# Shorter first passes over two blocks, one stay for the sigmoids, and a reordered opening

## The chip, the core and the metric

The kernel runs on one core of a Trainium2 chip. The metric is the device time of one execution in microseconds (us). A core has a matrix engine (PE, with PEld for its weight loads), a vector engine (DVE), an activation engine (ACT), GpSimd (POOL) and a queue engine (SP) that issues the DMAs. Every engine works through its own list of instructions in order; they meet only at semaphores. A difference of about 2% (9 us) is what is called a change in the verdicts.

## The reference

An attention of the mLSTM kind over 768 steps for 2 batches and 8 heads of width 40 gives 1536 rows of 320 numbers. Two feed-forward layers of width 2048 follow, each with its own weights:

```python
h_tilde = np.einsum('bhde,bhe->bhd', C, qt)
denom = np.maximum(np.abs(nq), 1.0)
o = 1.0 / (1.0 + np.exp(-o_gate[:, :, t]))
y[:, :, t] = o * h_tilde / denom
...
h = x @ w_in
g = h - np.tanh(h)            # layer 1
x = g @ w_out
...
h = x @ w_in
g = h * np.tanh(log1p(exp(h)))  # layer 2
return g @ w_out
```

## The kernel before

The 1536 rows are twelve tiles of 128, in six blocks of two. The 2048 columns of a layer are 16 weight parts of 128. A part comes in by DMA as `raw` and is made ready by `conv_w` in six passes: on DVE a shift (L198), on ACT the sign (a Prelu, L206), on DVE a shift-and-or (L210), on ACT the high half (L213), on DVE the low half (L215, L216). Every product uses high and low halves, so the first product of one part for one block is 8 matmuls of 256 columns (L538, tile `h`), and the second is 6 matmuls of 320 columns (L598, L599, L600, tile `acc`): `gh` times the high weights, `gh` times the low, and `gl` times the high.

Two parts make a tile of work (`tile1`). ACT takes two Tanh of `h` (L560, L561), a Square (L562), a Relu (L565) and the rounded half `gh` (L549); DVE makes `g` (L563), `t` (L564) and a predicated copy (L566); POOL makes `gl` (L550).

Layer 1 visits every block twice. The first pass over block n uses `CUT[n]` parts, starting as soon as the attention of that block is done, and while it runs the attention of block n+1 is computed beside it. After the sixth block a second pass visits each block with the parts that are left. What a first pass leaves out, the second does: the sum of matmuls doesn't depend on `CUT`. Layer 2 follows.

The attention of a row tile j goes: `nb` (PE) to an Exp (`Dm`, ACT L340), a mask (POOL L342), scores `sc` (PE), their product (DVE L362), `it` and `pv` (PE L369, L380), then DVE's sums and the gate (L374 to L394). L393 multiplies by the sigmoid of the output gate, which `session` puts on ACT (L259); the Sigmoid needs another activation table than the Exp, and so a table load (ACT_TABLE_LOAD) on either side. The gated rows `xo` are transposed (`xt`, PE L283), and ACT and DVE make the halves of `xT` (L285, L286), which the first products of that block read. Below, "a" and "b" are the two row tiles of block 1, and parts and tiles of work are counted from 0.

The order on each engine comes from a scheduler that ranks ready instructions by its own timing model; `with after(...)` only puts an instruction behind another. In the opening, where PE would stand idle, `keep(n, x)` puts n filler matmuls (`w_ps`, L639) behind x.

Of the kernel before, what the change touches and what calls it, by code (L numbers as in the profile page):

```python
# [8 lines left out]
F32 = mybir.dt.float32  # L9
F32R = mybir.dt.float32r  # L10
U32 = mybir.dt.uint32
AF = mybir.ActivationFunctionType
# [13 lines left out]
def kernel(  # L26
# [54 lines left out]
    NB = len(blocks1)  # L81


    CUT = [8] + [10] * (NB - 1)
    M1 = max(BLOCKS) * L
    M2 = max(len(x) for x in flat) * L
    MX = max(NP * M1, M2)
# [38 lines left out]

    last, chain, fill, mark, second = [], [], [], [], []

    texp, tbl, dls, tanhs = [], [], [], []

    scored, gated, rounded, relus = {}, {}, {}, {}

# [24 lines left out]
    def copy_r(eng, o, x):  # L157
        if eng == 0:
            nc.scalar.activation(out=o, in_=x, func=AF.Copy)
        elif eng == 1:  # L160
            nc.vector.tensor_copy(o, x)
        else:
            nc.gpsimd.tensor_scalar(o, in0=x, scalar1=1.0, scalar2=0.0, op0=ALU.mult, op1=ALU.add)
# [6 lines left out]
    def load_w(n=1):  # L170
        for _ in range(n):
            if pending_loads:
                layer, f = pending_loads.pop(0)
                early = layer == 0 and f < ER
                t = (xp if early else rawp).tile(
                    [P, 2 * WC], U32, tag="x" if early else "raw", name="raw", bufs=NB - 1 if early else None
                )
                queued(
                    lambda: nc.sync.dma_start(out=t, in_=(w1, w2)[layer][f].bitcast(U32)), layer == 0 and f < CUT[0]
                )  # L180
                raw[layer, f] = t
# [3 lines left out]
    def conv_w(layer, f, first=(), behind=()):  # L185
        r = raw.pop((layer, f)).rearrange("p (n t) -> p n t", t=2)
        lo32, z = r[:, :, 0], r[:, :, 1]
        zf = z.bitcast(F32)
        w = wp.tile([P, WT], F32R, tag="w", name="w")
        wf = w.bitcast(F32)  # L190

        head = texp if (layer, f) == (0, 0) else tanhs if layer == 0 and f < CUT[0] else []
        if layer == 0 and f:
            head = head + [scaled[0, f - 1]]
        with after(first):
            nc.vector.tensor_scalar(lo32, in0=lo32, scalar1=29, scalar2=None, op0=ALU.logical_shift_right)  # L198
        if second:
            nc.vector.scalar_tensor_tensor(  # L200
                lo32, in0=z, scalar=0x80000000, in1=lo32, op0=ALU.bitwise_and, op1=ALU.bitwise_or
            )
            scaled[layer, f] = nc.scalar.activation(out=zf, in_=zf, func=AF.Copy, scale=2.0 ** -111)
        else:
            with after(head):
                scaled[layer, f] = nc.scalar.activation(  # L206
                    out=zf, in_=zf, func=AF.Prelu, scale=2.0 ** -111, alpha=-2.0 ** 32
                )
        with after(behind):
            third[layer, f] = nc.vector.scalar_tensor_tensor(  # L210
                z, in0=z, scalar=3, in1=lo32, op0=ALU.logical_shift_left, op1=ALU.bitwise_or
            )
        cvd[:] = [nc.scalar.activation(out=w[:, 0:WC], in_=zf, func=AF.Copy)]  # L213
        eng = nc.gpsimd if (layer, f) == (0, 0) else nc.vector
        eng.tensor_tensor(w[:, WC:WT], in0=zf[:, 0:REM0], in1=wf[:, 0:REM0], op=ALU.subtract)  # L215
        lows[layer, f] = eng.tensor_tensor(w[64:P, REM0:REM1], in0=zf[64:P, REM0:REM1], in1=wf[64:P, REM0:REM1], op=ALU.subtract)  # L216
        wtile[layer, f] = w
# [60 lines left out]
    def transpose_x(layer, bi, pos):  # L278
        j = blk[layer, bi][pos]
        src = xo[:, j, :]  # L280
        t_ps = at_ps([P, 3, P], "xt")
        for n in range(3):
            x = nc.tensor.transpose(t_ps[:, n, :], src[:, n * P:(n + 1) * P], ident)  # L283
        hi, lo = (t[:, :, pos * L:(pos + 1) * L] for t in xT[layer, bi])
        chain[:] = [x, nc.scalar.activation(out=hi, in_=t_ps, func=AF.Copy)]  # L285
        chain.append(nc.vector.tensor_tensor(lo, in0=t_ps, in1=hi.bitcast(F32), op=ALU.subtract))  # L286

    def trans(layer, bi):
        new_xT(layer, bi)
        for n in range(len(blk[layer, bi])):  # L290
            transpose_x(layer, bi, n)
            yield

    def keep(n, x):
        if fill:
            fill[0](n, [x])

    def attention(j):
# [80 lines left out]
        for h in range(H):  # L379
            x = nc.tensor.matmul(pv[:, h, :], lhsT=Dm[:, h, :], rhs=v[:, h, :], start=True, stop=True)  # L380
        if not j:
            keep(2, x)
        if c > 0:
            nc.vector.tensor_tensor(hv, in0=hv, in1=pv, op=ALU.add)
        else:
# [13 lines left out]
        if c + 1 < NCH:  # L399
            st = at_ps([P, HG, D1], "st")  # L400
            with in_turn(first=chain[:1] if c == 0 else ()) as turn:
                for h in [HG * r + g for g in range(HG) for r in range(2)]:
                    turn(lambda: nc.tensor.matmul(hp(st, h), lhsT=k[:, h, :], rhs=wv[:, h, :], start=True, stop=True))
            for r in range(2):
                sl = slice(HP * r, HP * r + D)
                if c == 0:
                    copy_r(0, C[sl, :, r, :], st[sl])
                else:
                    dc = dec[sl, b, :, c:c + 1].to_broadcast([D, HG, D1])
                    nc.gpsimd.tensor_tensor(C[sl, :, r, :], in0=C[sl, :, r, :], in1=dc, op=ALU.mult)  # L410
                    nc.vector.tensor_tensor(C[sl, :, r, :], in0=C[sl, :, r, :], in1=st[sl], op=ALU.add)
# [141 lines left out]
    def tile1(i):  # L553
        l, bi, fs, nt = span(i)
        n = len(fs) * nt
        h = hps.pop(i)
        u, t, g = (g2.tile([P, MX], F32, tag=nm, name=nm)[:, 0:n] for nm in "utg")

        with after([scaled[0, fs[-1] + 1]] if i < CUT[0] // NP - 1 else []):
            nc.scalar.activation(out=u, in_=h, func=AF.Tanh, scale=G_B)  # L560
            tanhs[:] = [nc.scalar.activation(out=t, in_=h, func=AF.Tanh)]  # L561
        nc.scalar.activation(out=u, in_=u, func=AF.Square, scale=G_SA)  # L562
        mark[:] = [nc.vector.tensor_tensor(g, in0=u, in1=h, op=ALU.mult)]  # L563
        nc.vector.tensor_tensor(t, in0=h, in1=t, op=ALU.subtract)  # L564
        relus[i] = nc.scalar.activation(out=u, in_=u, func=AF.Relu, bias=bias[:, 0:1])  # L565
        nc.vector.copy_predicated(out=g, mask=u.bitcast(U32), data=t)  # L566
        split_g(i, g, n)
# [64 lines left out]
    def program():  # L632
# [64 lines left out]
        def go(g, n=1):  # L697
            for _ in range(n):
                next(g, 0)
# [2 lines left out]
        rest = rest()  # L702
        go(gb, 4)
        go(ga)
        transpose_x(0, 0, 0)
        go(gb)
        keep(4, chain[0])
        transpose_x(0, 0, 1)
        go(ga)
        go(gb)  # L710
        load_w(2)
        loads_to(2 * B, "qk")
        load_w(1)
        loads_to(2 * B, "kv")
        load_w(1)
        start = chain[:]
        conv1 = [0]

# [10 lines left out]
                conv1[0] += 1  # L729

        lead1(PRE)
        rest = rest()
        rest = rest()
        at_pools[:] = [(ps_acc, "acc")] * PS[0] + [(ps_at, "at")] * PS[2]
# [2 lines left out]
        def attend():  # L737
            for k in range(1, NB):
                js = blk[0, k]
                gens = [(n, attention(j)) for n, j in enumerate(js)]  # L740
                if k < NB - 1:
                    new_xT(0, k)
                loads_to(js[0] + 1)
                while gens:
                    for n, g in list(gens[:2]):
                        loads_to(js[n] + 2)
                        if next(g, 0) == 0:
                            gens.remove((n, g))
                            if k < NB - 1:
                                yield  # L750
                                transpose_x(0, k, n)
                        yield
            left.close()
            late["x"] = pool(left, "lateX", 1, reuse_waits="tile")
            late["A"] = pool(left, "lateA", 2, reuse_waits="tile")
            yield from trans(0, NB - 1)
# [35 lines left out]
        n_s = CUT[0] // NP  # L792


        CY, R2, E2 = 6, 3, 6

        def conv_to(i, bi, f):
            if i < n_s:
# [12 lines left out]
        for i in range(len(tiles)):  # L811
# [28 lines left out]
            mm1(i)  # L840
            if l == 0:
                tile1(i)
                if 1 < i < 4:
                    session(2 * i - 3, 2 * i - 1 + (i > 2), i == 3, [cvd[0], relus[2]] if i < 3 else [rounded[2], relus[3], rounded[3]])
                qm.append(i)
                if len(qm) > LAG:
                    mm2(qm.pop(0))
                if i:
                    ahead(min(int(14 * (k + (i - i0 + 1) / n_seg + 0.4)), (8, 14)[i - 1] if i < 3 else 14 * NB))
                if k >= T2:  # L850
                    next(sg, None)
                    next(sg, None)
            else:
                tile2(i)
                qm.append(i)
                if len(qm) > LAG2:
                    mm2(qm.pop(0))
                next(sg, None)
# [66 lines left out]
```

## Time and profile before

| | us |
|---|---|
| three runs | 457.56, 459.34, 546.25 |
| their median | 459.34 |
| the profiled execution | 457.39 |
| its span, first to last instruction | 455.4 |
| PE busy | 444.0 (97%) |
| PE's filler matmuls, 45 of them | 14.7 |
| DVE busy | 299.9 (66%) |
| ACT busy | 284.2 (62%) |

The run of 546.25 is a stray one and is not compared with. The profiled execution's time is 1.99 us above its span. Busy times are sums over one engine, so they overlap between engines; PE's contains the fillers. The granted clock is what PE ran at as a share of 2.4 GHz: 1.00 is 2.4 GHz and 0.50 is 1.2 GHz.

### The profile page before, as it was taken

To read this page: it belongs to the slowest core of one execution; us is meant where nothing else is said; L and a number is where in the kernel's file an instruction comes from. 1 tells how busy PE (TensorE), PEld (TensorE's weight loads), DVE (VectorE), ACT (ScalarE), POOL (GpSimd) and SP (SyncE) were. 2 spreads that over 40 slices of the span, in tenths; PEclk is the share of its full clock that TensorE was granted. 3 is DMA by queue.
4 is the path that set the end of the run, shared out by engine and by line. 5 is a ranking of instruction groups with operands and counts; after the bars stand their busy time and mean duration, and the time that the engine had idled before them with its cause. 6 is when DMAs were issued, how large, how long until landed. Compare 5 with 4: busy or idle time off the path is not lost. (4 is left out here: it accounts for less than half of the span.)

```text
span 455.4 us, 7958 instructions
## 1 busy us (share of the span) xinstructions
PE 444.0 (97%) x3099; PEld 403.0 (88%) x3099; DVE 299.9 (66%) x524; ACT 284.2 (62%) x519; POOL 105.1 (23%) x119
## 2 busy tenths in 40 slices
PE   9989989999999999999999999999999999999997
PEld 5756979989989999999999989999989899898996
DVE  7889889948988687568799986989622212211112
ACT  6679798568584866789778877676533332322331
POOL 2305534433464421243323332000000000000000
PEclk9799999999999999999999999999999999999999
DMA  7984644531344310001111110435010000010001
GB/s 239 374 286 163 184 108 139 167 97 47 105 131 123 94 64 1 1 2 63 65 65 63 65 64 1 134 121 189 2 59 0 1 0 2 15 44 0 1 0 58
DMA packets 22728, 38.03 MB, mean 84 GB/s; under 512 B 1348, under 2 KB 17028, under 8 KB 22692
## 3 DMA queue, kind: packets, MB, share of 16 engines
q1 hardware_dynamic: 22692, 37.54, 25.7%
q8 instruction: 24, 0.39, 0.4%
q14 instruction: 12, 0.10, 0.1%
HBM read 35.41 MB, written 1.97 MB: 82 GB/s over the span
## 5 line engine op out<-in xcount | busy, mean ns | idle before, releaser
L538 PE MATMUL h<-xT,w 128*128 128x256 f32 (+1 forms) x1152 | 205.9, 321 | 4.9 <-ACT w L213 1.9
L538 PEld LDWEIGHTS h<-xT,w 128*128 128x128 f32 x1152 | 167.9, 189 | 21.9 <-ACT w L213 2.3
L598 PE MATMUL acc<-w,gh 128*128 128x320 f32 x384 | 119.7, 313 | 0.5 <-DVE xo L615 0.5
L599 PE MATMUL acc<-w,gh 128*128 128x320 f32 x384 | 118.8, 310 | 0.0
L600 PE MATMUL acc<-w,gl 128*128 128x320 f32 x384 | 114.8, 312 | 0.0
L550 POOL TENSOR_TENSOR gl<-g,gh 128x512 fp32r<-128x512 f32 x48 | 64.4, 1343 | 132.4 <-ACT gh L549 132.1
L579 DVE TENSOR_TENSOR gl<-g,gh 128x512 fp32r<-128x512 f32 x48 | 33.2, 691 | 88.1 <-ACT g L578 88.0
L577 ACT ACTIVATE gh<-h 128x512 fp32r<-128x512 f32 x48 | 28.8, 600 | 75.4 <-PE h L538 75.3
L598 PEld LDWEIGHTS acc<-w,gh 128*128 128x128 f32 x384 | 72.2, 188 | 3.0 <-ACT u L562 0.7
L599 PEld LDWEIGHTS acc<-w,gh 128*128 128x128 f32 x384 | 72.2, 188 | 2.4
L600 PEld LDWEIGHTS acc<-w,gl 128*128 128x128 f32 x384 | 70.3, 188 | 1.0 <-POOL Dm L342 0.4
L563 DVE TENSOR_TENSOR g<-u,h 128x512 f32<-128x512 f32 x48 | 32.8, 684 | 25.2 <-ACT u L562 16.9
L566 DVE COPY_PREDICATED g<-u,t 128x512 f32<-128x512 uint32 x48 | 40.1, 843 | 12.8 <-ACT u L565 12.7
L549 ACT ACTIVATE gh<-g 128x512 fp32r<-128x512 f32 x48 | 30.4, 634 | 18.9 <-DVE g L566 17.1
L565 ACT ACTIVATE u<-u,bias 128x512 f32<-128x512 f32 x48 | 34.7, 726 | 6.9 <-DVE g L563 6.8
L213 ACT ACTIVATE w<-raw 128x704 fp32r<-128x704 f32 x32 | 27.3, 860 | 15.0 <-DVE raw L210 14.8
L564 DVE TENSOR_TENSOR t<-h,t 128x512 f32<-128x512 f32 x48 | 32.9, 685 | 0.0
L560 ACT ACTIVATE u<-h 128x512 f32<-128x512 f32 x48 | 28.6, 595 | 4.1 <-PE h L538 3.7
L562 ACT ACTIVATE u<-u 128x512 f32<-128x512 f32 x48 | 30.5, 639 | 0.0
L210 DVE SCALAR_TENSOR_TENSOR raw<-raw 128x704 uint32<-128x704 uint32 x32 | 29.1, 921 | 0.5
L561 ACT ACTIVATE t<-h 128x512 f32<-128x512 f32 x48 | 28.8, 599 | 0.0
L578 ACT ACTIVATE g<-h 128x512 f32<-128x512 f32 x48 | 28.6, 596 | 0.0
(104 smaller groups left out, 452.5 us busy)
## 6 DMA issues: line engine op xcount, KB each, us to landing
raw<-in_w_dram SPq DMA_DIRECT2D x32, 704.0 KB
qk_t<-in_qk_dram SPq DMA_DIRECT2D x12, 512.0 KB
kv_t<-in_kv_dram SPq DMA_DIRECT2D x12, 324.0 KB
out_dram<-xo SPq DMA_DIRECT2D x12, 160.0 KB
xo<-in_og_dram SPq DMA_DIRECT2D x2, 800.0 KB
xo<-in_og_dram SPq DMA_DIRECT2D x1, 320.0 KB
sd<-nr SPq DMA_DIRECT2D x20, 4.0 KB
md<-nr SPq DMA_DIRECT2D x10, 8.0 KB
```

Of the source, the lines that this page charges most:

```text
L538: y = nc.tensor.matmul(t[:, k * nt:(k + 1) * nt], lhsT=w[:, o:o + P], rhs=x[:, kk, :], start=(n == 0), stop=(n == len(pairs) - 1),)
L549: rounded[i] = nc.scalar.activation(out=gh, in_=g, func=AF.Copy)
L550: nc.gpsimd.tensor_tensor(gl, in0=g, in1=gh.bitcast(F32), op=ALU.subtract)
L562: nc.scalar.activation(out=u, in_=u, func=AF.Square, scale=G_SA)
L563: mark[:] = [nc.vector.tensor_tensor(g, in0=u, in1=h, op=ALU.mult)]
L564: nc.vector.tensor_tensor(t, in0=h, in1=t, op=ALU.subtract)
L565: relus[i] = nc.scalar.activation(out=u, in_=u, func=AF.Relu, bias=bias[:, 0:1])
L566: nc.vector.copy_predicated(out=g, mask=u.bitcast(U32), data=t)
L579: mark.append(nc.vector.tensor_tensor(gl, in0=g, in1=gh.bitcast(F32), op=ALU.subtract))
L598: turn(lambda: nc.tensor.matmul(a, lhsT=gh[:, sl], rhs=wh, start=(f in ends_), stop=False))
L599: turn(lambda: nc.tensor.matmul(a, lhsT=gh[:, sl], rhs=wl, start=False, stop=False))
L600: turn(lambda: nc.tensor.matmul(a, lhsT=gl[:, sl], rhs=wh, start=False, stop=end))
```

## The change

The first pass over block 0 uses 6 parts where it used 8, the one over block 1 uses 8 where it used 10 (`CUT`); the second pass takes over the difference. The pace at which later parts are converted starts from 4 where it started from 6 (`CY`). The five later sigmoids, which stood in two calls of `session` behind tiles 2 and 3, stand in one call behind tile 2, each behind another instruction of ACT. In the opening, three fillers stand behind the first `pv` where there were two; the sign pass of a part stands behind the Square of the tile, where it stood behind the second Tanh; the low half of the first `xT` waits for the gated rows of the second row tile; the copies of the state `C` stand behind the conversion of part 1; and the rest of block 0's attention is written after the conversion of the first two parts.

```diff
-    CUT = [8] + [10] * (NB - 1)
+    CUT = [6, 8] + [10] * (NB - 2)
...
-        head = texp if (layer, f) == (0, 0) else tanhs if layer == 0 and f < CUT[0] else []
+        head = texp if (layer, f) == (0, 0) else squared if layer == 0 and f < CUT[0] else []
...
-        chain.append(nc.vector.tensor_tensor(lo, in0=t_ps, in1=hi.bitcast(F32), op=ALU.subtract))
+
+        def low():
+            chain.append(nc.vector.tensor_tensor(lo, in0=t_ps, in1=hi.bitcast(F32), op=ALU.subtract))
+
+        return low
...
-            keep(2, x)
+            keep(3, x)
...
-                    copy_r(0, C[sl, :, r, :], st[sl])
+                    with after(cvd):
+                        copy_r(0, C[sl, :, r, :], st[sl])
...
-            tanhs[:] = [nc.scalar.activation(out=t, in_=h, func=AF.Tanh)]
-        nc.scalar.activation(out=u, in_=u, func=AF.Square, scale=G_SA)
+            nc.scalar.activation(out=t, in_=h, func=AF.Tanh)
+        squared[:] = [nc.scalar.activation(out=u, in_=u, func=AF.Square, scale=G_SA)]
...
-        transpose_x(0, 0, 0)
+        low = transpose_x(0, 0, 0)
         go(gb)
         keep(4, chain[0])
-        transpose_x(0, 0, 1)
-        go(ga)
-        go(gb)
-        load_w(2)
-        loads_to(2 * B, "qk")
-        load_w(1)
-        loads_to(2 * B, "kv")
-        load_w(1)
+        with after([gated[1]]):
+            low()
+        transpose_x(0, 0, 1)()
...
         lead1(PRE)
+        go(ga)
+        go(gb)
+        load_w(2)
+        loads_to(2 * B, "qk")
+        load_w(1)
+        loads_to(2 * B, "kv")
+        load_w(1)
...
-        CY, R2, E2 = 6, 3, 6
+        CY, R2, E2 = 4, 3, 6
...
-                if 1 < i < 4:
-                    session(2 * i - 3, 2 * i - 1 + (i > 2), i == 3, [cvd[0], relus[2]] if i < 3 else [rounded[2], relus[3], rounded[3]])
+                if i == 2:
+                    session(1, NCH, True, [cvd[0], rounded[1], relus[2], rounded[2], rounded[2]])
```

In the changed kernel the line numbers after the first edits are 4 to 7 higher (L538 is L543, L598 is L603, L380 is L384, L562 is L567).

On ACT, around the sigmoids (`xo<-xo`) of tile 2, which is `u_590` and `gh_600` before, and `u_573` and `gh_583` after. Before, from the Square of tile 2 to its `gh`:

```order
L562 ACTIVATE u_590<-u_590 128x512
L213 ACTIVATE w_551<-raw_335 128x704
L549 ACTIVATE gh_515<-g_507 128x512
L340 ACTIVATE Dm_445<-nb_454 128x512
L213 ACTIVATE w_560<-raw_467 128x704
L259 ACT_TABLE_LOAD
L259 ACTIVATE xo_91<-xo_91 128x2x320
L565 ACTIVATE u_590<-u_590,bias_89 128x512
L259 ACTIVATE xo_91<-xo_91 128x2x320
L549 ACTIVATE gh_600<-g_592 128x512
```

After, the same stretch:

```order
L554 ACTIVATE gh_516<-g_508 128x512
L567 ACTIVATE u_573<-u_573 128x512
L344 ACTIVATE Dm_446<-nb_455 128x512
L259 ACT_TABLE_LOAD
L259 ACTIVATE xo_91<-xo_91 128x2x320 x2
L570 ACTIVATE u_573<-u_573,bias_89 128x512
L259 ACTIVATE xo_91<-xo_91 128x2x320
L554 ACTIVATE gh_583<-g_575 128x512
L259 ACTIVATE xo_91<-xo_91 128x2x320 x2
```

The two high halves of parts 6 and 7 (L213) are gone from the stretch, and two sigmoids where there was one stand ahead of tile 2's Relu.

On PE, at `pv` of block 1 (`pv_627` and `pv_651` before, `pv_614` and `pv_638` after); `gl_601` before and `gl_584` after are the low half of tile 2. Before:

```order
L598 MATMUL acc_606<-w_460,gh_600 128x320
L599 MATMUL acc_606<-w_460,gh_600 128x320
L598 MATMUL acc_607<-w_460,gh_600 128x320
L599 MATMUL acc_607<-w_460,gh_600 128x320
L380 MATMUL pv_627<-kv_t_331,Dm_436 128x41 x8
L369 MATMUL it_645<-C1_99,qk_t_327 128x82 x4
L380 MATMUL pv_651<-kv_t_333,Dm_445 128x41 x8
L600 MATMUL acc_606<-w_460,gl_601 128x320
L600 MATMUL acc_607<-w_460,gl_601 128x320
```

After:

```order
L605 MATMUL acc_594<-w_470,gl_584 128x320
L384 MATMUL pv_614<-kv_t_346,Dm_437 128x41 x8
L373 MATMUL it_632<-C1_99,qk_t_342 128x82 x4
L384 MATMUL pv_638<-kv_t_348,Dm_446 128x41 x8
L407 MATMUL st_655<-wv_520,kv_t_346 40x41 x8
L283 MATMUL xt_668<-ident_88,xo_91 128x128 x3
L407 MATMUL st_674<-wv_534,kv_t_348 40x41 x8
L283 MATMUL xt_687<-ident_88,xo_91 128x128 x2
L341 MATMUL nb_766<-md_96,sd0_94 128x512
L341 MATMUL nb_775<-md_96,sd1_95 128x512
```

All second products of block 0 now stand ahead of both `pv`, the eight that need `gl_584` or follow one that does among them; behind the second `pv` none is left.

On DVE, from the last gated rows of block 1 (L394 before, L398 after) to the second low half of its `xT` (L286, now L288). Before, where `raw_476` and `raw_558` are parts 8 and 9:

```order
L394 SCALAR_TENSOR_TENSOR xo_91<-xo_91,den_661 128x320
L198 TENSOR_SCALAR raw_476<-raw_476 128x704
L198 TENSOR_SCALAR raw_558<-raw_558 128x704
L411 TENSOR_TENSOR C1_99<-C1_99,st_687 40x4x41 x2
L210 SCALAR_TENSOR_TENSOR raw_476<-raw_476 128x704
L210 SCALAR_TENSOR_TENSOR raw_558<-raw_558 128x704
L286 TENSOR_TENSOR xT_429<-xt_681,xT_429 128x3x128
L286 TENSOR_TENSOR xT_429<-xt_700,xT_429 128x3x128
```

After, where `raw_350` and `raw_468` are parts 6 and 7:

```order
L398 SCALAR_TENSOR_TENSOR xo_91<-xo_91,den_648 128x320
L198 TENSOR_SCALAR raw_350<-raw_350 128x704
L198 TENSOR_SCALAR raw_468<-raw_468 128x704
L210 SCALAR_TENSOR_TENSOR raw_350<-raw_350 128x704
L210 SCALAR_TENSOR_TENSOR raw_468<-raw_468 128x704
L215 TENSOR_TENSOR w_693<-raw_350,w_693 128x576
L216 TENSOR_TENSOR w_693<-raw_350,w_693 64x128
L288 TENSOR_TENSOR xT_430<-xt_687,xT_430 128x3x128
```

The first low half of `xT` and the state's sums moved ahead of the gated rows, and part 6's low half (L215, L216) came in ahead of the second low half of `xT`.

## Rows read from the trace of the kernel before

**Rows 1.** Windows view, PE alone: stretch, its length, busy (instructions), granted clock, DMA, GB/s.

```profile
0.00:65.00 65.00, 59.16 (x425) 0.95 0.72 235
65.00:160.00 95.00, 94.02 (x813) 1.00 0.37 110
```

**Rows 2.** Windows view, PE alone, in half microseconds of the opening.

```profile
16.50:17.00 0.50, 0.50 (x5) 0.50 1.04 405
...
23.00:23.50 0.50, 0.50 (x5) 0.80 0.98 380
```

**Rows 3.** Timeline of PE, opening: start, length, instructions [idle before, and whom it waited for].

```profile
15.09 2.50 PE L380 MATMUL pv<-kv_t,Dm 128*128 128x41 f32 x16
...
18.21 1.89 PE L639 MATMUL w_ps<-const-bfloat16-1.0 128*32 128x512 bf16 x4
20.03 0.90 PE L283 MATMUL xt<-ident,xo 128*128 128x128 f32 x3
...
22.11 1.69 PE L538 MATMUL h<-xT,w 128*128 128x256 f32 x8
...
38.42 1.20 PE L538 MATMUL h<-xT,w 128*128 128x256 f32 x8
```

**Rows 4.** Timeline of ACT: sign pass and Square of tile 0; then sigmoids and tile 2.

```profile
27.38 0.82 ACT L206 ACTIVATE raw<-raw 128x704 f32<-128x704 f32 x1
28.10 0.63 ACT L562 ACTIVATE u<-u 128x512 f32<-128x512 f32 x1
...
45.47 1.28 ACT L259 ACT_TABLE_LOAD   x1
46.77 0.74 ACT L259 ACTIVATE xo<-xo 128x640 f32<-128x640 f32 x1
47.41 0.71 ACT L565 ACTIVATE u<-u,bias 128x512 f32<-128x512 f32 x1
...
50.11 0.63 ACT L549 ACTIVATE gh<-g 128x512 fp32r<-128x512 f32 x1 [1.36 <-DVE g L566]
```

**Rows 5.** Timeline of DVE: tiles 0 and 1, then the last xT of block 1 and part 8.

```profile
28.75 0.69 DVE L563 TENSOR_TENSOR g<-u,h 128x512 f32<-128x512 f32 x1 [1.19 <-ACT u L562]
...
41.82 0.74 DVE L566 COPY_PREDICATED g<-u,t 128x512 f32<-128x512 uint32 x1
...
61.18 0.68 DVE L411 TENSOR_TENSOR C<-C,st 40x164 f32<-40x164 f32 x2
61.89 1.70 DVE L210 SCALAR_TENSOR_TENSOR raw<-raw 128x704 uint32<-128x704 uint32 x2
63.62 1.02 DVE L286 TENSOR_TENSOR xT<-xt,xT 128x384 fp32r<-128x384 f32 x2
64.56 0.76 DVE L215 TENSOR_TENSOR w<-raw,w 128x576 fp32r<-128x576 f32 x1
65.33 0.29 DVE L216 TENSOR_TENSOR w<-raw,w 64x128 fp32r<-64x128 f32 x1
```

**Rows 6.** The page's costliest groups: the high half of a part; count, busy us, mean ns.

```profile
L213 ACT ACTIVATE w<-raw 128x704 fp32r<-128x704 f32 x32 | 27.3, 860 | 15.0 <-DVE raw L210 14.8
```

**Rows 7.** Timeline of POOL: the low half of tile 2.

```profile
50.82 1.29 POOL L550 TENSOR_TENSOR gl<-g,gh 128x512 fp32r<-128x512 f32 x1 [2.85 <-ACT gh L549]
```

**Rows 8.** Timeline of PE: end of block 0's first pass, start of block 1's, start of block 2's.

```profile
51.86 1.87 PE L380 MATMUL pv<-kv_t,Dm 128*128 128x41 f32 x16
...
64.23 0.96 PE L337 MATMUL nb<-md,sd 128*128 128x512 f32 x3 [0.79 <-DVE xT L286]
65.03 3.66 PE L538 MATMUL h<-xT,w 128*128 128x256 f32 x30
...
86.08 0.31 PE L599 MATMUL acc<-w,gh 128*128 128x320 f32 x1
86.23 0.31 PE L600 MATMUL acc<-w,gl 128*128 128x320 f32 x1
...
94.69 0.98 PE L538 MATMUL h<-xT,w 128*128 128x256 f32 x6 [0.42 <-ACT xT L285]
```

More of the change, by code (lines that the diff above doesn't have):

```diff
@@ L127 @@
     last, chain, fill, mark, second = [], [], [], [], []
-    texp, tbl, dls, tanhs = [], [], [], []
+    texp, tbl, dls, squared = [], [], [], []
     scored, gated, rounded, relus = {}, {}, {}, {}
@@ L290, in trans @@
         for n in range(len(blk[layer, bi])):
-            transpose_x(layer, bi, n)
+            transpose_x(layer, bi, n)()
             yield
@@ L750, in attend @@
                                 yield
-                                transpose_x(0, k, n)
+                                transpose_x(0, k, n)()
                         yield
```

## The prediction

> **What bounds the kernel now.** I read the page's busy shares first, then PE in stretches, then the timelines of PE, ACT, DVE and POOL before 66 us. From 65 to 160 us PE is busy 94.02 of 95 us, and before 65 us 59.16 of 65 [rows 1]; a good part of that is filler (14.7 us over the span, in the table), and some at half clock. So PE sets the end from 65 us on, and work moved from one pass to another behind that point costs nothing and gives nothing. What can change the time is how much useful PE work is done when PE starts to run without a stop. In the kernel before that point is 65.03 us: eight parts of block 0 are done, and the first products of block 1 run on [rows 8]. The measure is therefore this: when does the changed kernel reach the same state, and how much PE work does it then still owe?
>
> **What it owes.** Two parts of block 0 go to the second pass. A first product is 8 matmuls a part; thirty of them took 3.66 us, 0.12 each [rows 8], so 16 are 1.9 us. A second product is 6 a part, 0.147 us apart (86.08 to 86.23) [rows 8]; 12 are 1.76. The debt is 3.65 us, paid later at PE's full pace. The two parts that block 1 gives up are the same trade once more, but PE is already busy there, so they cost nothing unless something they covered comes late (the second rival).
>
> **The opening up to tile 0.** I take DVE's first g (L563) as the mark: 28.75 us, where DVE had waited 1.19 us for the Square on ACT [rows 5]. The sign pass stood ahead of that Square and held it 0.72 us (27.38 to 28.10) [rows 4]; behind it, the Square starts that much earlier. Against this stands the third filler: four took 1.89 us at half clock, 0.47 each, and 0.24 at full clock [rows 3], and the second pv stands behind it. On the path I take 0.24, since at that place the clock is still full. The changed order of xT's low half and the gated rows on DVE would bring the second transpose earlier, but the four fillers end at 18.21 + 1.89 = 20.10 and the transpose begins at 20.03 [rows 3], so as long as the clock is low there the fillers hold it. The mark moves by -0.72 + 0.24, about -0.5, to 28.25 us. Bounds: +0.24 if the sign pass finds another thing in its way (part 2's high half follows it), and -1.9 in the first rival.
>
> **From the mark to the end of tile 2.** Times from here are counted from the mark. Before, ACT's table load for the sigmoids comes at 16.7 (45.47), tile 2's Relu at 18.7 (47.41), its gh at 21.4 (50.11) [rows 4], its gl on POOL from 22.1 to 23.4 [rows 7], and the first pv of block 1 at 23.1 (51.86) [rows 8]. Parts 6 and 7 take from ACT two sign passes (0.72 each, as above) and two high halves (0.86, of which about 0.1 overlaps the next, so 0.76 [rows 6]): 3.0 us, all ahead of the table load. The load comes at 13.7. From it to the first sigmoid are 1.30 us and from one sigmoid to the next instruction 0.64 [rows 4]; two sigmoids now stand ahead of the Relu, so it starts at 13.7 + 1.3 + 1.3 = 16.3 where one would have made it 15.7. The Relu is 0.71 [rows 4], the predicated copy on DVE behind it 0.74 [rows 5], and DVE has nothing else queued there any more (parts 6 and 7 were what made this step 2.7 us before). So gh comes at 17.8, gl at 17.8 + 0.7 = 18.5, and 1.29 later, at 19.8, PE can go on.
>
> Here the order on PE has changed. Before, pv came ahead of the second products that need this gl; now all of them come ahead of it. The first gl product and the seven behind it are 8 x 0.147 = 1.2 us, so the first pv starts at 21.0, and not at about 18 where its data would have been ready. That is 2.1 us earlier than before, of the 3.6 that gh gained. DVE is relieved of part 6 and part 7 too, but since ACT is the longer chain here that buys nothing of its own.
>
> **From pv to running on.** Before, this took 65.03 - 51.86 = 13.2 us [rows 8]. Of the work on DVE behind pv, tile 3's predicated copy (0.74) is gone, and the state's sums (0.68) and the first low half of xT (half of 1.02) now fill a wait ahead of the last gated rows [rows 5]. Part 6's low half came in ahead of the second low half of xT: 0.76 + 0.29 [rows 5]. 13.2 - 0.74 - 1.2 + 1.05 = 12.3. Laying out the whole list with the durations before gives 11.9, and nothing gained would be 13.2; I take 12.3 and keep both ends. The six first products that need only the high half are in the gap in both kernels. PE runs on at 21.0 + 12.3 = 33.3 behind the mark, at 28.25 + 33.3 = 61.55 us.
>
> **The sum.** 65.03 - 61.55 = 3.5 us earlier, with 3.65 us of work still owed: a loss of 0.15 us. The later edits cost nothing by themselves: the number of sigmoids and of their table loads (two either way) stays, `CY` only shifts conversions that ACT and DVE can place beside a PE that is full [rows 1], and the copies of the state stand in ACT's list ahead of a Square that waits for PE in any case. Against the profiled execution, 457.39 us, the sum is 457.5. That execution lies 0.17 under the lower of the two comparable runs and 1.95 under the other, so I add 0.3 us for where a median falls: **457.8 us**, which is no change.
>
> **Rivals.** *First: the third filler keeps the clock up.* The granted clock was 0.50 from about 16.5 us until 23 us [rows 2]. It fell during the second pv, matmuls of 41 columns that load PE little [rows 3], with two fillers ahead of them; a third is what the change adds there. For it speaks that the eight first products took 1.69 us there and 1.20 at full clock [rows 3], so there is something to win; against it, that one filler is a small addition. If the clock stays, the four fillers end near 19.0 instead of 20.1, the transpose then follows the gated rows (at 19.2), and the first products of part 0 come 1 us earlier and end 1.4 us earlier. The mark goes to 26.9: 1.35 us more than above, 456.4 us.
>
> *Second, and slower: PE waits so long at the end of block 0's first pass that its clock falls there.* After the second pv nothing is left of block 0 to fill with: from pv's end to the run of first products, some 7 us, PE has `st`, `xt` and four `nb`, about 3 us of work, and no fillers. Before, second products stood on both sides of pv, and `nb` waited only 0.79 us [rows 8]. In the opening the clock fell during just such thin work, and stayed down for 6.5 us [rows 2]. If it falls here, the first products that follow run at half clock: of 3 to 6.5 us of such work half is lost, 1.5 to 3.2 us (an estimate from the 6.5 us of [rows 2], up to half of which would fall into the wait itself). That gives 459.3 to 461.0; it decides as soon as the clock is at 0.50 when block 1's run begins.
> The Trainium skill speaks for this rival (TensorE: Matmul & The Clock Gate, section "HAM oscillation — how this bites in real kernels"): waits between bursts of matmuls throttle PE again, and the next burst starts cold. The trace agrees only in the opening; at 62 to 65 us, where the wait was short, no row shows a fall.
>
> *Third: the shorter pass over block 1 no longer covers the attention of block 2.* Two parts are 3.65 us of cover. At the start of block 2 PE waited 0.42 us for xT on ACT [rows 8], so the chain beside it ended about when PE's work did; if the chain is as long as before, PE waits up to 3.65 us more. Against it: the chain has one tile fewer (five to four) to share ACT and DVE with. Price 1 to 3.65 us, 458.8 to 461.5.
>
> *Fourth: the wait at pv is not real,* because gl comes earlier than I have it and the chain from pv is shorter by up to 2 us: 455.8.
>
> **How the numbers follow.** An even exchange, 456.8 to 458.8: 0.45. Clock held in the opening: 0.22. Clock lost at the end of the first pass: 0.15. Cover gone in block 1: 0.13. Shorter chain: 0.05. To hold 8 in 10 the range takes in the even exchange, the clock held with the shorter tail (456.4 less 1.4 for 11.9 instead of 13.2 counted at both places, 455.0) and most of the two slower cases: 454.8 to 461.3. A difference of 2%, 9.2 us, is about what a measurement of this kernel tells from no change, and none of these cases reaches it alone: faster by more than 2% 0.03, within 2% 0.94, slower 0.03.
>
> **What would show it.** In the changed kernel: the mark (first L568 on DVE) at 28.2, or near 27 if the clock held; the clock between 16.5 and 23 us; tile 2's gh some 17.8 us behind the mark and the first pv of block 1 21 behind it, idle before it on POOL's gl; the first products of block 1 running on at 61 to 62 us; the clock there; and PE's idle time at the start of block 2. I am wrong if the run begins before 60 us, if pv doesn't wait for gl, or if PE shows new idle time behind 65 us.

## The result: 1.3% slower, where no change was predicted

The changed kernel took 464.41 us (median of four runs, 462.39 to 465.85). Three comparable runs of the kernel before, beside it on the same chip, took 457.37, 457.56 and 459.34. The ratio is 1.0132, with a 95% interval of 1.0100 to 1.0163. That is less than the 2% that a verdict asks for, but 6.6 us over the predicted 457.8, and above the range (to 461.3). The profiled execution took 464.9, with a span of 463.0: 7.6 more than before. A stray run, 545.14 us in e8 below as 546.25 before, is in no ratio, but e8's median of 457.27 has one in it and is 457.03 without.

In the changed kernel the lines are L543 for `h`, L603 to L605 for `acc`, L384 for `pv`, L407 for `st`, L341 for `nb`, L568 for `g`, L554 for `gh`, L555 for `gl` and L644 for the fillers.

First PE in stretches (the view of [rows 1] and [rows 2]: stretch, length, busy and instructions, granted clock, DMA, GB/s):

```profile
16.00:24.00 8.00, 6.74 (x71) 1.00 1.06 339
24.00:30.00 6.00, 4.33 (x30) 1.00 0.80 251
30.00:34.00 4.00, 3.88 (x12) 0.57 0.85 253
...
55.00:58.00 3.00, 1.19 (x34) 0.98 0.94 257
58.00:62.00 4.00, 3.01 (x7) 0.50 0.22 86
62.00:66.00 4.00, 3.77 (x16) 0.50 0.35 85
66.00:70.00 4.00, 4.00 (x30) 0.73 0.74 273
70.00:75.00 5.00, 5.00 (x47) 1.00 0.03 12
```

Before, the clock was low once, from 16.5 to 23 us [rows 2], and PE was nearly full from 65 us on [rows 1]. Now the clock holds in the opening, and is low at two other places: at 30 to 34 us, and from 58 us to about 68, after PE had been idle for more than half of 55 to 58.

The timeline of PE (start, length, instructions, idle time before and whom it waited for), against [rows 3] and [rows 8]:

```profile
31.07 2.31 PE L644 MATMUL w_ps<-const-bfloat16-1.0 128*32 128x512 bf16 x5
33.31 1.50 PE L543 MATMUL h<-xT,w 128*128 128x256 f32 x8
...
47.52 1.12 PE L373 MATMUL it<-C,qk_t 128*128 128x82 f32 x8
48.44 0.39 PE L603 MATMUL acc<-w,gh 128*128 128x320 f32 x1
...
49.11 0.46 PE L605 MATMUL acc<-w,gl 128*128 128x320 f32 x2
...
50.14 0.31 PE L605 MATMUL acc<-w,gl 128*128 128x320 f32 x1
50.28 1.87 PE L384 MATMUL pv<-kv_t,Dm 128*128 128x41 f32 x16
...
52.92 1.92 PE L384 MATMUL pv<-kv_t,Dm 128*128 128x41 f32 x16
...
58.78 0.66 PE L283 MATMUL xt<-ident,xo 128*128 128x128 f32 x2 [2.59 <-issue]
...
62.23 4.92 PE L543 MATMUL h<-xT,w 128*128 128x256 f32 x20 [0.33 <-ACT xT L285]
...
77.27 1.87 PE L384 MATMUL pv<-kv_t,Dm 128*128 128x41 f32 x16
...
92.06 1.04 PE L341 MATMUL nb<-md,sd 128*128 128x512 f32 x2 [1.44 <-issue]
92.94 0.86 PE L543 MATMUL h<-xT,w 128*128 128x256 f32 x6
...
181.03 0.42 PE L603 MATMUL acc<-w,gh 128*128 128x320 f32 x1 [1.72 <-ACT gh L554]
```

The first `pv` of block 1 stands right behind the last second product of block 0; tile 2's twelve took PE from 48.44 to 50.28 us. PE wasn't idle ahead of them, and the first product that needs `gl` began at 49.11, 0.24 us behind the end of `gl` (48.87, from the POOL line below). Twenty first products take 4.92 us at 62.23 where thirty took 3.66 before [rows 8]. "Issue" at 58.78 means that the profile names no releaser. The timeline of DVE, which makes the gated rows that `xt` transposes, gives one:

```profile
27.68 0.69 DVE L568 TENSOR_TENSOR g<-u,h 128x512 f32<-128x512 f32 x1 [0.27 <-ACT u L567]
...
52.20 0.50 DVE L388 TENSOR_TENSOR hv<-hv,pv 128x328 f32<-128x328 f32 x1 [3.00 <-PE pv L384]
...
58.19 0.49 DVE L398 SCALAR_TENSOR_TENSOR xo<-xo,den 128x320 f32<-128x320 f32 x1
```

DVE stood still for 3.00 us until `pv` came. Its chain from there ends with the gated rows at 58.68, and the `xt` starts 0.1 us later. ACT and POOL around tile 2, against [rows 4] and [rows 7], and on ACT the second high half of `xT`, for which PE waits at 62.23:

```profile
40.13 0.60 ACT L565 ACTIVATE u<-h 128x512 f32<-128x512 f32 x1 [1.02 <-PE h L543]
...
42.76 1.28 ACT L259 ACT_TABLE_LOAD   x1
...
45.33 0.71 ACT L570 ACTIVATE u<-u,bias 128x512 f32<-128x512 f32 x1
...
46.87 0.63 ACT L554 ACTIVATE gh<-g 128x512 fp32r<-128x512 f32 x1 [0.21 <-DVE g L571]
...
60.94 0.86 ACT L213 ACTIVATE w<-raw 128x704 fp32r<-128x704 f32 x1
61.68 0.50 ACT L285 ACTIVATE xT<-xt 128x384 fp32r<-128x384 f32 x1
```

```profile
47.58 1.29 POOL L555 TENSOR_TENSOR gl<-g,gh 128x512 fp32r<-128x512 f32 x1 [2.79 <-ACT gh L554]
```

### The profile page after: what moved, and what is told of

The parts are those of the page before. It is cut to its first block, busy times and chain, and to the rows that moved or that the text cites. A ratio compares the mean times of both kernels' runs of the same rounds, so it can differ in the third digit from the quotient of the medians.

```text
span 463.0 us, 7962 instructions
## 1 busy us (share of the span) xinstructions
PE 447.5 (97%) x3100; PEld 405.1 (87%) x3100; DVE 297.7 (64%) x524; ACT 284.6 (61%) x519; POOL 103.4 (22%) x119
## 4 chain that ended last, share of the span: by engine, by line
PE 74%; DVE 15%; ACT 6%; issue 3%; POOL 1%; ACTq 0%; DVEq 0%; POOLq 0%
PE h L543 32%; PE acc L603 10%; PE acc L605 10%; PE acc L604 10%; PE sc L362 4%; DVE g L571 2%; PE w_ps L644 2%; PE pv L384 2%; DVE raw L210 2%; DVE w L215 1%; DVE g L568 1%; DVE t L569 1%; DVE raw L198 1%; PE it L373 1%; ACT u L570 1%
## 5 line engine op out<-in xcount | busy, mean ns | idle before, releaser
L543 PE MATMUL h<-xT,w 128*128 128x256 f32 (+1 forms) x1152 | 207.8, 324 | 3.0 <-ACT w L213 1.6
L543 PEld LDWEIGHTS h<-xT,w 128*128 128x128 f32 x1152 | 170.3, 191 | 20.6 <-ACT w L213 1.7
L603 PE MATMUL acc<-w,gh 128*128 128x320 f32 x384 | 120.0, 314 | 2.5 <-ACT gh L554 1.7
L605 PE MATMUL acc<-w,gl 128*128 128x320 f32 x384 | 114.8, 312 | 0.0
L555 POOL TENSOR_TENSOR gl<-g,gh 128x512 fp32r<-128x512 f32 x48 | 64.3, 1340 | 129.9 <-ACT gh L554 121.2
L603 PEld LDWEIGHTS acc<-w,gh 128*128 128x128 f32 x384 | 72.1, 188 | 5.8 <-ACT gh L554 1.9
L605 PEld LDWEIGHTS acc<-w,gl 128*128 128x128 f32 x384 | 70.2, 188 | 1.1 <-issue 0.4
L571 DVE COPY_PREDICATED g<-u,t 128x512 f32<-128x512 uint32 x48 | 39.0, 813 | 20.7 <-ACT u L570 20.4
L554 ACT ACTIVATE gh<-g 128x512 fp32r<-128x512 f32 x48 | 30.4, 634 | 25.3 <-DVE g L571 19.8
L568 DVE TENSOR_TENSOR g<-u,h 128x512 f32<-128x512 f32 x48 | 32.6, 679 | 16.5 <-ACT u L567 10.6
L213 ACT ACTIVATE w<-raw 128x704 fp32r<-128x704 f32 x32 | 27.5, 859 | 10.2 <-DVE raw L210 9.5
L210 DVE SCALAR_TENSOR_TENSOR raw<-raw 128x704 uint32<-128x704 uint32 x32 | 31.1, 976 | 0.3
L567 ACT ACTIVATE u<-u 128x512 f32<-128x512 f32 x48 | 30.5, 635 | 0.0
```

The source lines that it names most:

```text
L210: third[layer, f] = nc.vector.scalar_tensor_tensor(z, in0=z, scalar=3, in1=lo32, op0=ALU.logical_shift_left, op1=ALU.bitwise_or)
L543: y = nc.tensor.matmul(t[:, k * nt:(k + 1) * nt], lhsT=w[:, o:o + P], rhs=x[:, kk, :], start=(n == 0), stop=(n == len(pairs) - 1),)
L555: nc.gpsimd.tensor_tensor(gl, in0=g, in1=gh.bitcast(F32), op=ALU.subtract)
L567: squared[:] = [nc.scalar.activation(out=u, in_=u, func=AF.Square, scale=G_SA)]
L603: turn(lambda: nc.tensor.matmul(a, lhsT=gh[:, sl], rhs=wh, start=(f in ends_), stop=False))
L605: turn(lambda: nc.tensor.matmul(a, lhsT=gl[:, sl], rhs=wh, start=False, stop=end))
```

## The experiments

The theory that I took into them (A): PE comes late to the run of block 1 and at half clock, because nothing of block 0 is left to fill its wait. The main rival (B): the new opening and the one stay of the sigmoids cost the time, and the shorter passes don't. A further question was what the shorter pass over block 1 adds by itself. All ratios are to runs of the kernel before on the same chip, whose medians were 457.85 for the first eight kernels and 457.59 for the last three. Theory C, in the expectations below, is that the shorter passes cost by the cover that is missing. That the order on PE at `pv` makes the wait is a theory that formed only on the way; e8 is its test.

**e1: the shorter passes alone**, in the kernel before.

```diff
-    CUT = [8] + [10] * (NB - 1)
+    CUT = [6, 8] + [10] * (NB - 2)
...
-        CY, R2, E2 = 6, 3, 6
+        CY, R2, E2 = 4, 3, 6
```

> The kernel before with the shorter first passes alone (6, 8, then 10 parts, pace 4); the opening, the sign pass and the sigmoids as before. Theory A, that the short passes leave PE waiting at the end of block 0's pass and that its clock falls there: as slow as the whole change, 462 to 466 us, with the granted clock at 0.50 for some 6 us or more when block 1's run begins. Theory B, that the edits of the opening and the sigmoids in one stay cost the time: 457 to 459 us, no fall of the clock at 55 to 70 us.

468.55 us, 1.0236 [1.0191, 1.0281], above the range that A gave. The shorter passes alone cost 10.7 us, and the rest of the change gives some 4 to 5 of them back (1.0236 against 1.0132): B is false.

**e2: the changed kernel with the old passes** (8 parts, then 10; `CY` 6).

> The changed kernel with the first passes as they were (8, then 10 parts, pace 6); all its other edits stay. Theory A: the slowdown is gone, and the earlier first g on DVE (27.7 us against 28.75) shows as about 1 us of gain: 456.5 to 458.5 us, clock 1.00 at 55 to 70 us. Theory B: still slow, 462 us or more.

457.65 us, 1.0002 [0.9982, 1.0022]. With the old passes, the opening, the one stay and the sign pass together neither give nor cost anything. But the clock, expected at 1.00, was down here too, behind 2.2 us of idle time on PE (56.47 to 58.65):

```profile
58.00:62.00 4.00, 3.35 (x28) 0.70 0.13 21
62.00:66.00 4.00, 2.97 (x16) 0.87 0.16 62
```

So a fall of the clock at this place, as long as this one, doesn't by itself make the loss.

**e3: twelve fillers in PE's wait**, behind the last `st` of block 1, in the changed kernel.

```diff
+    FILL = 12
...
+            if j == 3:
+                keep(FILL, pe[-1])
...
-            if i == n_s:
+            if i == n_s + 1:
```

The last two lines only let fillers stand for one tile of work longer.

> The changed kernel with 12 fillers more, on PE behind the last state product of block 1, where it stood idle for 2.6 us. The scheduler also puts the second low half of xT ahead of part 6's. Theory A: the clock stays at 1.00 when block 1's run begins; half of the 6 us of work that ran at half clock comes back, 3 us, and up to 1 us from the order on DVE: 460 to 462 us. If the clock there is not what costs (theory C, the shorter passes cost by the missing cover alone): 463 to 465 us, the fillers being free or a little dear.

460.00 us, 1.0044 [1.0018, 1.0069]. In the windows of this kernel the clock is no longer down behind 58 us, and PE's idle time now shows at 75 to 90 us:

```profile
58.00:62.00 4.00, 3.60 (x22) 1.00 0.05 17
62.00:66.00 4.00, 4.00 (x38) 1.00 0.33 71
...
75.00:90.00 15.00, 13.23 (x113) 1.00 0.39 108
```

Fillers do no work of the reference, and yet two thirds of the loss went, some 4 us (from 1.0132 to 1.0044). The scheduler also put the second low half of `xT` ahead of part 6's, and on ACT the second high half ahead of part 6's (59.91 against 61.12), so not all of it is shown to be the clock's.

**e4 and e5: ten parts for block 1's pass again** (`CUT` 6, then 10), without and with the twelve fillers.

> The changed kernel with the pass over block 1 back at 10 parts, block 0's at 6. Theory A: the loss is made at block 0's end, so 462.5 to 465 us; at most the PE wait of 1.4 us at the start of block 2 comes back, 463 us. Theory C, that the missing cover in block 1's pass is the larger part: 459 to 461 us.

> The 12 fillers behind block 1's last state product, with block 1's pass at 10 parts and block 0's at 6. If the two causes found so far (the clock at block 0's end, about 4 us; the shorter pass over block 1, about 4 us) are separate and add up: 464.4 - 4.4 - 4.0, 456 to 457.5 us, level with the kernel before or a little under it. If they are one and the same delay that each run hides in its own way: 459 to 460.5 us.

460.38 [1.0038, 1.0085] and 459.18 [1.0017, 1.0070]. By the ratios the fillers alone (e3) give 4.0 us, the longer pass alone 3.3, and both together 4.1: they are not two separate prices. e4's result fell into theory C's range (459 to 461), but e5's is the one expected of a single delay. In e4 the clock was still 0.50 from 58 to 66 us, with the same 2.59 us ahead of `xt`.

**e6: twelve fillers with the old passes**, e2 with e3's edit.

> The same 12 fillers with the first passes as before the change (8 and 10 parts). In the run without them the clock was 0.70 at 58 to 62 us and 0.87 at 62 to 66 us. If the clock is dear wherever it falls: 456 to 457 us, 1 us less than without. If only PE work that sets the end counts, and there is little of it there: 457.5 to 459 us.

459.53, 1.0054 [1.0031, 1.0076]: 1.9 us more than e2's median and above both ranges expected. The fillers came behind PE's idle time, not into it: they ran from 60.23 us, took 4.45 us at half clock, and seven second products waited behind them. Here they only delay.

**e7: eight parts for both blocks** (`CUT` 8, 8, then 10; `CY` 6).

> The changed kernel with 8 parts over block 0 and over block 1: block 1's shorter pass by itself. If missing cover costs there by itself (theory C): 2 to 4 us over the run with 8 and 10 parts, 459.7 to 461.7 us, with PE idle at the start of block 2. If the shorter pass hurts only behind a late start of block 1 (theory A): 457 to 458.5 us.

458.90, 1.0020 [0.9995, 1.0045], 1.2 us over e2's median, between the two ranges expected, and its interval takes in no change. So block 1's shorter pass costs little where block 0 keeps its eight parts.

**e8: `pv` first.** The changed kernel, with the second products of tile 2 held behind block 1's second `pv`. PE does the same work, nearly in the order of before at this place (there four of tile 2's second products stood ahead of `pv`).

```diff
...
+        if j == 3:
+            late_pv[:] = [x]
...
-                    turn(lambda: nc.tensor.matmul(a, lhsT=gh[:, sl], rhs=wh, start=(f in ends_), stop=False))
+                    with after(late_pv if i == 2 else []):
+                        turn(lambda: nc.tensor.matmul(a, lhsT=gh[:, sl], rhs=wh, start=(f in ends_), stop=False))
```

> The changed kernel with the twelve second products of tile 2 held behind block 1's second pv, so that pv goes ahead of them and they stand where PE was idle. If the order on PE is what made the wait (the step of the prediction that has pv wait for gl): pv starts 2 us earlier, the twelve fill the gap behind it, the clock stays up or falls later, 458.5 to 461 us. If the wait is the attention's own chain: pv earlier but block 1's run not, and 463 to 465 us.

457.27 us, 0.9984 [0.9957, 1.0010]: all of the loss is gone, some 7 us, and more than was expected (458.5 to 461). In this kernel the lines are L545 for `h` and L606 to L608 for `acc`. Its timeline of PE:

```profile
45.59 1.92 PE L384 MATMUL pv<-kv_t,Dm 128*128 128x41 f32 x16
...
48.27 1.92 PE L384 MATMUL pv<-kv_t,Dm 128*128 128x41 f32 x16
50.02 0.39 PE L606 MATMUL acc<-w,gh 128*128 128x320 f32 x1
...
54.49 0.97 PE L545 MATMUL h<-xT,w 128*128 128x256 f32 x6 [0.58 <-ACT xT L285]
...
57.29 1.90 PE L545 MATMUL h<-xT,w 128*128 128x256 f32 x14
```

and its windows:

```profile
30.00:34.00 4.00, 4.00 (x23) 1.00 0.93 328
...
55.00:58.00 3.00, 2.49 (x14) 1.00 0.15 53
58.00:62.00 4.00, 4.00 (x36) 1.00 0.47 128
62.00:66.00 4.00, 4.00 (x43) 1.00 0.65 245
```

DVE's first `g` and tile 2's `gh`, as marks for the times below:

```profile
26.30 0.69 DVE L570 TENSOR_TENSOR g<-u,h 128x512 f32<-128x512 f32 x1 [0.29 <-ACT u L569]
```

```profile
44.08 0.63 ACT L556 ACTIVATE gh<-g 128x512 fp32r<-128x512 f32 x1 [0.19 <-DVE g L573]
```

The second products now lie between `pv` and the first products, beside DVE's chain, where they fill. The first twenty first products are done at 59.19 us, against 67.15. About 1.4 us of that difference is this execution's earlier opening (DVE's first `g` at 26.30 against 27.68). The scheduler moved more along with them: the second high and low halves of `xT` stand ahead of part 6's again (on ACT 53.95 against 56.76, on DVE 56.68 against 57.64), and of what DVE had ahead of the last gated rows (two pairs of the state's sums and the first low half of `xT`) only one pair of sums is left there. e8 doesn't part these from the order on PE.

**e9: `pv` first with 6 and 10 parts**, e8 with e4's cut.

> The changed kernel with block 1's second pv ahead of tile 2's second products, and with ten parts for block 1's first pass again (6, 10). If block 1's shorter pass has a price of its own, as the kernel with 8 and 8 parts hinted (about 1.2 us over the one with 8 and 10), this one takes 456.1 us, against 457.3 with pv ahead and 6 and 8 parts. If that price was only PE's wait at the start of block 2 in a pass that began late, there is none left now: 457.3, within 0.6. In both cases PE's clock is 1.00 from 55 us to 75 us, since the order at pv is the same. It is over 458.5 only if the order at pv doesn't carry over to this cut.

457.46, 0.9984 [0.9961, 1.0006]. With `pv` first, block 1's shorter pass is free. What e4 gained over the changed kernel was part of the same delay, not a price of its own.

**e10: the shorter passes alone, `pv` first**, e1 with e8's edit.

> The kernel before with the shorter passes alone (6, 8 parts, slower pace of conversion), where the sigmoids stay in two calls and the opening is the old one, and with block 1's second pv ahead of tile 2's second products. Without the last it took 468.6 us. If the order at pv is what costs here too, it comes down by 5 to 8 us, to 461 to 463.5, with the clock at 1.00 between 55 and 66 us, and the rest of some 4 us to the changed kernel with pv ahead (457.3) is what the sigmoids' one stay and the opening are worth. If its price lies elsewhere (PE idle 66 to 75 us, where it stood still for about half of the time), it stays at 466 to 468.

465.93, 1.0184 [1.0149, 1.0218]: 2.6 us under e1's median, where 5 to 8 were expected, and the two intervals overlap. Most of e1's loss has another cause. The clock held to 66 us, as expected, and was 0.59 from 66 to 70. The timelines of ACT and PE:

```profile
63.04 0.82 ACT L206 ACTIVATE raw<-raw 128x704 f32<-128x704 f32 x1 [2.26 <-DMA raw<-in_w_dram]
63.77 0.61 ACT L564 ACTIVATE u<-u 128x512 f32<-128x512 f32 x1
...
70.04 1.28 ACT L693 ACT_TABLE_LOAD   x1
```

```profile
65.84 3.66 PE L540 MATMUL h<-xT,w 128*128 128x256 f32 x16 [2.69 <-DVE t L566]
...
72.07 0.50 PE L337 MATMUL nb<-md,sd 128*128 128x512 f32 x1 [1.76 <-ACT Dm L340]
```

With six parts, tile 3 is block 1's first, and the second call of the sigmoids, which hangs on it, falls into that pass. Its table load at 70.04 stands ahead of block 2's Exp, for which PE waits 1.76 us; and a Square (63.77) waits behind a sign pass whose weights have not landed. That is read from this one trace, and I ran no kernel to part the two. It fits that the changed kernel, with one stay behind tile 2, is 4 us faster than e1.

**e11: two fillers in the opening**, e8 with `keep(2, x)` where the change has `keep(3, x)`.

> The changed kernel with block 1's second pv ahead of tile 2's second products, and with two fillers behind the first pv of the opening where it has three. If the third filler keeps the clock up in the opening (the prediction's first rival, 1.35 us), this one takes 458.6 us and the clock falls to 0.50 between 16.5 and 23 us. If the clock there falls or holds for another reason, the filler is worth its own 0.24 us or nothing: 456.9 to 457.4, and DVE's first g comes at 27.4 to 27.7 us.

457.41, 0.9982 [0.9959, 1.0006]. The windows, DVE's first `g` and tile 2's `gh`:

```profile
17.00:20.00 3.00, 3.00 (x10) 0.50 1.08 338
```

```profile
27.68 0.69 DVE L570 TENSOR_TENSOR g<-u,h 128x512 f32<-128x512 f32 x1
```

```profile
45.43 0.63 ACT L556 ACTIVATE gh<-g 128x512 fp32r<-128x512 f32 x1 [0.19 <-DVE g L573]
```

The clock fell in the opening, and the first `g` came 1.38 us later than in e8. But 0.75 of that was there at the first `pv` of the opening (12.29 against 11.54 us), which stands ahead of the fillers; counted from it, the fall, with one filler less, delays `g` by 0.6. The ratios are the same within 0.0002. That doesn't show the fall to be free, since the executions of one kernel differ in their mean granted clock: of e11's, four had 0.992, as the profiled one, and took 456.43 to 456.70; of e8's, three had 1.00, as its profiled one, and took 455.06 to 456.27. A fall in the opening seems to cost about 1 us of the time.

## Why the prediction was wrong

**What failed is the sum of the likeliest case: it counted the second products ahead of `pv` as 1.2 us on the path, and let PE run at full clock behind the wait that this order makes.** In its place the runs showed tile 2's twelve ahead of `pv`, 1.8 us; PE idle for 2.59 us behind it, where they had filled; and the twenty first products at half clock, 2.5 us lost. With the twelve behind `pv` all of some 7 us is gone (e8). The second rival, the clock that falls at the end of block 0's first pass, had 0.15 and came true in kind, but not in its price: it ended at 461.0. That nothing is left of block 0 to fill with stood in that rival, but not in the sum.

Point by point, in the changed kernel's trace:

- *The debt*, 3.65 us: it stands, and no run contradicts it. With `pv` first it is paid by earlier work (e8, e9: no difference from before).
- *The mark*: 27.68 us, predicted 28.25. Right in direction. Its first rival's premise came true in this trace, since the clock was 1.00 from 16 to 24 us with three fillers. The mark of 26.9 that went with it did not: counted from the opening's first `pv` (12.93 us, before 12.65), it came 1.35 us earlier than before, where 0.5 was predicted and 1.85 with that rival. A fall in the opening seems to cost about 1 us at the end (e11). That the third filler is what holds the clock isn't shown: e1 and e10, with two, also had 1.00 in that stretch.
- *The chain to tile 2's `gh`*: predicted 17.8 behind the mark, measured 19.2 (46.87). The working was right for full clock: in e8 it is 44.08 less 26.30, 17.8, and in e11 45.43 less 27.68, also 17.8; both had the clock at 1.00 from 24 to 36 us. In the changed kernel it fell at 30 to 34, five fillers took 2.31 us and eight `h` 1.50, and ACT waited 1.02 for tile 2's `h`. Sized wrong by 1.4, by a fall that I had not looked for there.
- *The first `pv`*: predicted 21.0 behind the mark, waiting for `gl`; measured 22.6, which is the 1.4 once more and 0.2. The wait for `gl` is not in the trace: PE was busy all the way, and what stood ahead of `pv` was the twelve products, 1.84 us. The prediction called this a sign of being wrong. In e8 `pv` comes at 19.3. The order on PE (1.9) and the clock at 30 to 34 us (1.4) together held it up by 3.3 us. The fourth rival is false, since `gl` ended 21.2 behind the mark and not before 19.8.
- *From `pv` to the run*: predicted 12.3, measured 11.95 (62.23 less 50.28). But six first products did not fit into the gap as I had said, since the second high half of `xT` ended only just before 62.23: 0.7 us more is owed. On ACT it stood behind an Exp pair and part 6's high half (60.94), though its `xt` was done at 60.50; the prediction had looked at that order on DVE alone.
- *The clock at the run*: the twenty first products took 4.92 us, where 20 at 0.122 [rows 8] are 2.44. That is 2.5 us lost, inside the second rival's 1.5 to 3.2. The Trainium skill's rule that was named for it (TensorE: Matmul & The Clock Gate, "HAM oscillation — how this bites in real kernels": waits between bursts throttle PE and the next burst starts cold) agrees with this trace, where 0.50 follows the idle time at 56 to 58.7 us, and with e3, where fillers in that wait leave 1.00. The opening of the kernel before, which the prediction gave as agreeing, is no such case: PE was busy in all of the half microsecond in which the clock is first down [rows 2], and in all of 10 to 20 us.
- *Cover in block 1*, the third rival: at the start of block 2 PE waited 1.44 us (92.06), 1.0 more than before [rows 8], the low end of its price. With the 1.72 us at 181.03 this is the new idle time behind 65 us that the prediction named as a sign of being wrong. But e8 is idle for 1.09 us of 75 to 90, where its block 2 begins, and e9, which has the longer pass, is no faster. So this wait is there and doesn't decide.

Against the predicted span (455.5, which is 457.5 less 1.99) the trace has 7.5 us more: 0.7 for the later run, 0.7 for the six products, 2.5 for the twenty at half clock, 0.5 for the 1.0 us at half clock that follow them (the 0.73 at 66 to 70 us), 1.0 at block 2's start, and 1.7 at 181.03, in a stretch in which PE was always busy before. That makes 7.1.

Against e8, counted from each kernel's first `g`, the twenty first products end 6.6 us later (67.15 less 27.68, and 59.19 less 26.30): 1.4 from the clock at 30 to 34 us, 1.9 from `pv` behind the twelve, 2.5 from the clock at the run, and 0.8 for the six products and the gap. But e8's profiled execution is its fastest, and the two lie 9.8 us apart (464.9 and 455.06), more than the medians. Of that, 1.4 is the earlier opening and 1.4 the fall at 30 to 34 us, which comes and goes between executions; the three other terms are 5.2 of the 7 us that are left, and the rest arises behind 67 us.

The fall at 30 to 34 us does seem to cost at the end. In e9's profiled execution it is the only one (0.86 over 24 to 36 us), and the mean granted clock is 0.996. Of e9's executions the eight with that mean clock took 457.78 us in the median, the four with 1.00 took 455.99. Where in the others the clock fell isn't recorded, so 1.8 us is an estimate from these two groups. In the changed kernel the one run at 0.989 took 462.39, the three at 0.982 to 0.985 took 463.93 to 465.85. Between e8 and the changed kernel lie some 7 us with it and without (464.9 against 457.59, the median of e8's six at 0.996, and 462.39 against 455.63, that of its three at 1.00), so, as far as the mean clocks tell, this fall doesn't make the loss.

Shown is that the order at `pv`, with what the scheduler moves along with it on ACT and DVE, carries the loss (e8, e9), and that fillers in PE's wait take more than half of it away (e3). Not settled is how it divides between the clock and the wait, since each remedy changes both; what the orders on ACT and DVE alone would cost; and what the wait at 181.03 hangs on: e8, which is idle for 1.22 us of 160 to 250, has its waits at other places.

Nothing here beats the kernel before: the best three, e8, e9 and e11, lie between 0.9982 and 0.9984, with intervals that take in 1.

## What to carry to other kernels

When the order on an engine changes, look at what the moved work covered, and not only at how long it takes: twelve second products ahead of `pv` delayed it and left the chain behind it bare, some 7 us in all, and the same twelve behind it cost nothing. Compare executions before traces: two profiled ones can lie further apart than the medians. An idle gap on PE can be charged twice, as idle time and in the clock of the work behind it.

## What the runs showed of the hardware

The clock fell at 30 to 34 us (0.57) in the changed kernel, with PE busy for 4.33 of the 6 us before; in e8, with 4.17 of the same 6 us, it stayed at 1.00. I had looked for a fall only in the opening and at the end of the pass. Whether it falls differs between executions of one kernel: e9's had mean clocks of 0.996 (eight) and 1.00 (four).

The Trainium skill says that PE's queue can pull weight loads ahead of matmuls in flight (TensorE: Matmul & The Clock Gate, "Architectural detail: the array is 16× 32×32, not 1× 128×128"). The trace agrees: the weights of `pv` were loaded from 50.14 us on, while the last second product ran (50.14 to 50.45). The `pv` itself stood in order behind the twelve: it began 2.76 us behind `it` (47.52 and 50.28), and 0.95 behind in e8 (44.64 and 45.59).
